# Quad 5 of a sigmoid attention: transposes by DMA in place of TensorE, an earlier load, and a counted order of matmuls

## The chip, the cores and the metric

The kernel runs on one core of a Trainium2 chip. The metric is the device time of one launch in microseconds. The times given for the kernel before are three runs: 369.92 us median, from 369.61 to 370.37. A profiled execution is a run of its own, with a record of every instruction; it took 369.69 us, of which 367.7 us lie between its first and last instruction (its span). Times inside a profile are counted from the start of the span.

## The reference

Two layers, one after the other. Inputs are q, k and v (8 batches, 12 heads, 448 positions, 64 wide), `w_in` (768 x 2048) and `w_out` (2048 x 768), all float32.

```python
scores = scale * np.matmul(q, k.transpose(0, 1, 3, 2)) - np.log(S)   # S = 448, scale = 1/8
attn = 1.0 / (1.0 + np.exp(-scores))
attn_out = np.matmul(attn, v)
x = attn_out.transpose(0, 2, 1, 3).reshape(B * S, H * D)             # 3584 x 768
h = x @ w_in
g = h * (1.0 / (1.0 + np.exp(-h)))
out = g @ w_out
```

The attention has no row sum, so every score goes through a sigmoid alone. Per batch that is a small attention (12 heads) and then two dense products over 448 rows.

## The kernel before, in words

Data is held in float16 on the chip, sums in float32 in PSUM.

**Quads, rounds and units.** Four heads of one batch are a quad; a batch has three (`NQ`), the kernel 24, numbered g = 0 to 23. Batch 0 is quads 0 to 2, batch 1 quads 3 to 5. A quad's scores are computed in seven rounds (`NCH`), each over 64 of its 448 key positions per head. A unit is one (quad, round) pair, numbered n = 7 g + round, so quad 5 has units 35 to 41. `scores` (L218) is one unit: four matmuls into a double PSUM bank and one sigmoid on ScalarE (L232). There are two such double banks. `values` (L240) is 28 matmuls for a quad over two single banks, and two scaled copies on VectorE (L267) into `xT`.

**Transposed q and k.** Scores need q and k with the head dimension on partitions (`kT`, `qT`). There are two ways in the code. `pe_transpose` (L188) multiplies by an identity on TensorE: 14 matmuls per tensor (L196) into two PSUM banks, and two casts on VectorE (L203). `dma_transpose` (L207) makes a row copy (`kr`, `qr`, L211) and lets SP issue a transposing DMA (L212). Quads 0 to 5 use the first, quads 6 to 23 the second.

**Loads.** POOL issues all loads of q, k, v, `w_in` and `w_out` in program order, with a cast from float32. At most eight are outstanding: each new one waits for the landing of the one eight before it. A tensor's buffer (three each for kf, qf, vf) must have been read before it is loaded again. `after_transpose(g)` (L633) and `after_values(g)` (L645) issue what follows a quad's transposes and values: after quad 1's transposes k and q of quad 4 and the first two quarters of `w_in`, after quad 2's k and q of quad 5, after quad 5's those of quad 8. A quarter of `w_in` is four transfers (L155) and 512 of its 2048 columns: h chunks 4 to 7 read the second quarter.

**h.** `h_unit` (L284) computes one chunk of 128 columns of h for a batch by six matmuls (L288) in a single bank. In batch 0 ScalarE then takes a sigmoid (L302) and VectorE multiplies (L303, this frees the bank); in batch 1 ScalarE takes one SiLU (L307). There are four single banks, which h, values and TensorE's transposes share. The bank that was released longest ago is taken.

**Order of the work.** The order on every engine is the order in which Python issues the calls. Units 0 to 23 follow a table (`behind`, L696). From unit 24 on (`NT_B + 3`) there are bursts of two units (L738), with the values of a finished quad behind them, and between bursts steps of h from the generator `first_h` (L551): all 16 chunks of batch 0, then of batch 1. How many steps follow a burst is set by a clock: `stretch(stream, 1600)` (L728) adds 1600 ns to what is due and takes steps, each 189 ns by the `yield 189` of `h_unit`, until they are used up. That makes 9, 8, 9, 8 and so on, 85 in all. Before that, four steps each of chunks 0 and 1 are done in the table. The values of quads 3, 4 and 5 come at burst 28, at burst 36 and behind the last burst. Quad 5's k is transposed behind burst 26, its q behind burst 30:

```python
    for n in range(NT_B + 3, 2 * NT_B, 2):
        burst(n)
        if n in (26, 30):
            transposes(5, "k" if n == 26 else "q")
        stretch(stream, 1600)
```

The rest of h for batches 0 and 1 follows without interruption, with sums of `w_in` and `w_out` pieces on VectorE between (L326, L477) and the row copies and DMA transposes of quads 6, 7 and 8. Then come the output products of batches 0 and 1 (`out_set`, L487) mixed with the attention of batches 2 and 3, and so on in pairs of batches.

Of the kernel before, what the change touches and what calls it, by code (L numbers as in the profile page):

```python
# [17 lines left out]
def kernel(  # L18
# [9 lines left out]
    nc = tc.nc  # L28
# [9 lines left out]
    NT_B = NQ * NCH  # L38
# [50 lines left out]
    def one_bank(name):  # L89
        if "any" in banks:  # L90
            ring.append(ring.pop(0))
            return banks["any"].tile([P, 512], F32, tag=f"any{ring[-1]}", name=name)
        taken["single"] += 1
        return banks["single"].tile([P, 512], F32, tag="single", name=name)
# [16 lines left out]
    def new_flat(name, g):  # L111
        flat[name, g] = p3.tile([P, 2, NCH, D], F16, tag=f"{name}f", name=f"{name}f")

    def rows_in(name, g):
        b, iq = divmod(g, NQ)
        return source[name][b, 4 * iq : 4 * iq + 4].rearrange(
            "(i h) (p c) d -> (h p) i (c d)", h=2, c=NCH
        )

    def load(names, g, c0=0, c1=NCH):  # L120
        for name in names:
            if (name, g) not in flat:
                new_flat(name, g)
            nc.gpsimd.dma_start(  # L124
                flat[name, g][:, :, c0:c1].rearrange("p i c d -> p i (c d)"),
                rows_in(name, g)[:, :, c0 * D : c1 * D],
            )
# [22 lines left out]
    def load_w_in(step):  # L150
        cols = slice(step * DFF // 4, (step + 1) * DFF // 4)
        rows = moe_w_in[:, cols].rearrange("(iq j h d) f -> h j d iq f", j=2, h=2, d=D)
        for half in range(2):
            for j in range(2):
                nc.gpsimd.dma_start(  # L155
                    w_in_sb[j * D : (j + 1) * D, half * NQ : (half + 1) * NQ, cols], rows[half, j]
                )
# [13 lines left out]
    def new_qkT(g):  # L171
        for name in ("k", "q"):
            qkT[name, g] = p3.tile([P, NCH, P], F16, tag=f"{name}T", name=f"{name}T")
# [14 lines left out]
    def pe_transpose(g, pieces=(("k", 0, 4), ("k", 4, NCH), ("q", 0, 4), ("q", 4, NCH))):  # L188
        if ("k", g) not in qkT:
            new_qkT(g)  # L190
        for name, c0, c1, *copy in pieces:
            dst = qkT[name, g].rearrange("p c t -> p (c t)")
            ptr = one_bank(f"ptr{name}")
            for c in range(c0, c1):
                for j in range(2):
                    nc.tensor.matmul(  # L196
                        ptr[j * D : (j + 1) * D, (c - c0) * P : (c - c0 + 1) * P],
                        flat[name, g][:, j, c, :],
                        ident,
                        start=True,  # L200
                        stop=True,
                    )
            (copy[0] if copy else nc.vector.tensor_copy)(  # L203
                dst[:, c0 * P : c1 * P], ptr[:, : (c1 - c0) * P]
            )

    def dma_transpose(g, name, copy):  # L207
        if ("k", g) not in qkT:
            new_qkT(g)
        rows = p2.tile([P, NCH, 2, D], F16, tag=f"{name}r", name=f"{name}r")  # L210
        copy(rows, flat[name, g].rearrange("p j c d -> p c j d"))  # L211
        nc.sync.dma_start_transpose(  # L212
            out=qkT[name, g], in_=rows.rearrange("p c j d -> p (c j d)")
        )
# [59 lines left out]
    def first_col(m):  # L274
        return P if m % 2 == 0 else 0

    def room_x():
        return p3.tile([P, NQ, S], F16, tag="tx", name="tx")
# [5 lines left out]
    def h_unit(b, fc):  # L284
        ph = one_bank("ph")
        for at, cc in enumerate(pairs):
            assert b in ready or at < 4
            nc.tensor.matmul(  # L288
                ph[:, :S],
                w_in_sb[:, cc, fc * P : (fc + 1) * P],  # L290
                xT[b][:, cc, :],
                start=(at == 0),
                stop=(at == NCC - 1),
            )
            if at < NCC - 1:
                yield 189
        if fc == NFC - 1:
            h_done.add(b)
        to = gTr[:, fc, first_col(0) + b * S : first_col(0) + (b + 1) * S]
        if b == 0:  # L300
            tsig = room_x()[:, 0]
            nc.scalar.activation(tsig, ph[:, :S], AF.Sigmoid, bias=0.0, scale=ISX)  # L302
            nc.vector.scalar_tensor_tensor(  # L303
                out=to, in0=ph[:, :S], scalar=ISX, in1=tsig, op0=ALU.mult, op1=ALU.mult
            )
        else:
            nc.scalar.activation(to, ph[:, :S], AF.Silu, bias=0.0, scale=ISX)  # L307
        yield 189
# [236 lines left out]

    by_h1 = {3: 6, 6: 7, 9: 8}
    early = [h_unit(0, fc) for fc in range(2)]
    sums = w_sums()
    in_sums = w_in_sums()

    def first_h():  # L551
        for b in range(2):
            for fc in range(NFC):
                yield from early[fc] if b == 0 and fc < 2 else h_unit(b, fc)
                if b == 0 and fc >= 10 or b == 1 and fc < 6:
                    next(in_sums)
                if b == 0:
                    continue
                if fc >= 2:
                    next(sums)  # L560
                if fc in by_h1:
                    for name in ("k", "q"):
                        dma_transpose(by_h1[fc], name, nc.vector.tensor_copy)
                    if by_h1[fc] == 8:

                        nc.gpsimd.tensor_copy(gate, qkT["q", 8][:1, 0, :1])
                        for to in (9, 10, 11):
                            load("kq", to)

    def sets(m):  # L570
        for g in range(0, NCH - 1, 2):
            step = out_set(
                block(m, g), row_blocks(m, g), block(m, g + 1), row_blocks(m, g + 1)
            )
            for i, ns in enumerate(step):
                if m == 0 and g == 0 and i in (10, 14):
                    next(sums)
                if m == 0 and g == 0 and i in (20, 28, 36, 44):
                    next(in_sums)
                yield ns  # L580
        if m % 2 == 1:
            g = NCH - 1
            yield from out_set(
                kept, row_blocks(m - 1, g), block(m, g), row_blocks(m, g), m == B // 2 - 1
            )
# [47 lines left out]
    def after_transpose(g):  # L633
        if g == 0:
            load("kq", 3)
        elif g == 1:
            load("kq", 4)
            load_w_in(0)
            load_w_in(1)
        elif g == 2:  # L640
            load("kq", 5)
        elif g == 5:
            load("kq", 8)

# [20 lines left out]
    def values_if_any():  # L665
        if waiting:
            g = waiting.pop(0)
            values(g)
            after_values(g)
            return True  # L670
        return False
# [6 lines left out]
    def rest_of_first_k():  # L678
        pe_transpose(0, (("k", FIRST, 4), ("k", 4, NCH)))
        after_transpose(0)  # L680

    def transposes(g, name):
        pe_transpose(g, ((name, 0, 4), (name, 4, NCH)))
        if name == "q":
            after_transpose(g)
# [37 lines left out]
        for do, *what in behind.get(n, ()):  # L723
            do(*what)

    done = due = 0.0

    def stretch(stream, ns, spent=0):  # L728
        nonlocal done, due
        due += ns  # L730
        done += spent
        while done < due:
            step_ns = next(stream, None)
            if step_ns is None:
                return
            done += step_ns

    def burst(n, size=2):  # L738

        new = units[n : n + size]  # L740
        for u in new:
            scores(*u)
        with_values = values_if_any()
        for g, ch in new:
            if ch == NCH - 1:
                waiting.append(g)
                if 9 <= g + 3 < NQB:
                    later.extend(((g + 3, "k"), (g + 3, "q")))
        return with_values

    stream = first_h()
    stretch(stream, 1600)
    for n in range(NT_B + 3, 2 * NT_B, 2):
        burst(n)
        if n in (26, 30):
            transposes(5, "k" if n == 26 else "q")
        stretch(stream, 1600)
    values_if_any()
    for _ in stream:
        pass  # L760
# [4 lines left out]
    for m in range(B // 2 - 1):  # L765
        banks_for_attention(3)
        nc.scalar.activation(warm, bias_s, AF.Sigmoid)
        stream = sets(m)
# [8 lines left out]
        left, n = 0.0, 2 * NT_B * (m + 1)  # L777
        for size in sizes * (2 * NQ):
# [3 lines left out]
            count = max(1, round(left / DENSE))  # L782
# [58 lines left out]
```

## Time and profile before

| | us |
|---|---|
| median of 3 runs | 369.92 |
| profiled execution | 369.69 |
| its span | 367.7 |
| 0 to 27.3: start, units 0 to 23 | 27.3, TensorE busy 24.3 |
| 27.3 to 56.6: bursts 24 to 40, values 3 to 5, h between | 29.3, TensorE busy 28.5, ScalarE 25.2 |
| 56.6 to 75.6: rest of h of batches 0 and 1 | 19.0, TensorE busy 18.9, VectorE 16.0 |
| 75.6 to 367.7: output products, attention and h of batches 2 to 7 | 292.1 |

The page names the engines PE (TensorE), DVE (VectorE), ACT (ScalarE), POOL and SP. A timeline row gives start, length, engine, line, instruction, what it writes and reads, and in brackets the idle time ahead of it with what ended that. A row of a view by windows gives the stretch, then each engine's busy time with the number of instructions, the granted clock of TensorE, the mean busy share of the 16 DMA engines (packets overlap, so that full engines show more than 1), and GB/s. A tile view gives the length of a DMA's issue and the time from the start of the issue to its landing.

### The profile page before, as it was taken

How to read it: one execution, taken by the hardware profiler on the slowest of the kernel's cores; microseconds unless marked ns; L12 is line 12 of the kernel's file. 1: busy time of each engine (PE TensorE's matmuls, PEld its weight loads, DVE VectorE, ACT ScalarE, POOL GpSimd, SP SyncE). 2: the span in 40 equal slices, each digit the busy share in tenths (PEclk: the TensorE clock that was granted, in tenths of full speed). 3: DMA queues.
4: the chain of work that ended last, by engine and by line, in shares of the span. 5: the costliest groups of instructions: out<-in, count | busy, mean ns of one | idle time of the engine just before them, and what ended most of it. 6: DMA issues, size and time to landing. Idle time of an engine off the chain costs nothing. (4 is left out here: it accounts for less than half of the span.)

```text
span 367.7 us, 7596 instructions
## 1 busy us (share of the span) xinstructions
PE 359.5 (98%) x3009; PEld 183.2 (50%) x3009; DVE 251.9 (68%) x458; ACT 249.9 (68%) x339; POOL 77.8 (21%) x116
## 2 busy tenths in 40 slices
PE   7999999999999999999999999999999999999995
PEld 2554445545544555544444545554455545555553
DVE  2565569867657587867665758795756667797763
ACT  5998885479998755687777846679998856640000
POOL 8566521040060172000051047000100000000000
PEclk9999999999999999999999999999999999999999
DMA  8999999989969499007589369912863020003333
GB/s 142 200 202 202 204 204 203 187 116 141 164 100 227 110 128 180 2 0 166 92 165 206 61 128 144 128 15 51 153 111 86 21 69 0 3 0 86 87 86 86
DMA packets 65698, 42.78 MB, mean 116 GB/s; under 512 B 36096, under 2 KB 62208, under 8 KB 65664
## 3 DMA queue, kind: packets, MB, share of 16 engines
q0 software_dynamic: 27072, 22.58, 42.3%
q1 hardware_dynamic: 38240, 19.44, 26.8%
q8 instruction: 23, 0.38, 0.4%
q10 hardware_dynamic: 352, 0.30, 0.2%
q14 instruction: 11, 0.09, 0.1%
HBM read 45.61 MB, written 11.01 MB: 154 GB/s over the span
## 5 line engine op out<-in xcount | busy, mean ns | idle before, releaser
L232 ACT ACTIVATE attnT<-psc,bias_s 128x896 f16<-128x896 f32 x168 | 158.1, 1009 | 21.9 <-PE psc L225 21.6
L504 PEld LDWEIGHTS <-S 128*128 128x128 f16 x448 | 41.3, 98 | 36.5 <-issue 8.1
L225 PE MATMUL psc<-qT,kT 64*64 64x448 f16 x672 | 51.1, 362 | 1.5 <-ACT qT L186 0.6
L267 DVE TENSOR_SCALAR xT<-pav 128x448 f16<-128x448 f32 x48 | 27.7, 620 | 33.2 <-PE pav L256 33.2
L124 POOL DMA_DIRECT2D vf<-in_v_dram x24 | 17.2, 717 | 135.0 <-PE pav L256 120.9
L504 PEld LDWEIGHTS <-gTr 128*128 128x128 f16 x336 | 31.3, 98 | 26.6 <-issue 7.7
L504 PE MATMUL po<-T,S 128*128 128x384 f16 x224 | 42.0, 327 | 0.2 <-DVE S L515 0.2
L504 PE MATMUL po<-w_out_sb,gTr 128*128 128x384 f16 x224 | 41.6, 327 | 0.0
L378 PEld LDWEIGHTS <-w_in_sb 128*128 128x128 f16 x288 | 27.7, 98 | 26.9 <-issue 1.7
L504 PE MATMUL po<-w_out_sb,S 128*128 128x384 f16 x224 | 40.8, 326 | 0.0
L256 PE MATMUL pav<-attnT,vf 64*64 64x448 f16 x672 | 38.9, 350 | 0.5 <-DVE gTr L303 0.4
L288 PE MATMUL ph<-xT,w_in_sb 128*128 128x448 f16 x192 | 38.7, 353 | 0.1
L378 PE MATMUL pa<-xT,w_in_sb 128*128 128x448 f16 x144 | 33.2, 353 | 0.0
L225 PEld LDWEIGHTS <-kT 64*64 64x64 f16 x672 | 17.8, 104 | 28.8 <-issue 22.3
L378 PEld LDWEIGHTS <-SI 128*128 128x128 f16 x216 | 21.1, 98 | 20.0 <-issue 0.5
L256 PEld LDWEIGHTS <-vf 64*64 64x64 f16 x672 | 21.0, 106 | 14.0 <-issue 4.7
L288 PEld LDWEIGHTS <-w_in_sb 128*128 128x128 f16 x192 | 17.8, 98 | 19.1 <-issue 3.7
L394 ACT ACTIVATE part<-pa 128x448 f32<-128x448 f32 x24 | 13.1, 544 | 19.9 <-PE pa L378 19.0
L504 PE MATMUL po<-T,gTr 128*128 128x384 f16 x112 | 22.1, 327 | 0.0
L372 ACT ACTIVATE gTr<-pc 128x448 f16<-128x448 f32 x24 | 13.1, 544 | 12.9 <-DVE pc L388 12.5
L388 DVE TENSOR_TENSOR part<-pb,part 128x448 f32<-128x448 f32 x24 | 14.9, 621 | 8.3 <-ACT part L394 5.0
L186 ACT ACTIVATE m<-po 128x384 f32<-128x384 f32 x1 | 0.5, 491 | 27.7 <-PE po L504 27.7
(75 smaller groups left out, 467.7 us busy)
## 6 DMA issues: line engine op xcount, KB each, us to landing
out_dram<-osb SPq DMA_DIRECT2D x54, 192.0 KB, 3.0
vf<-in_v_dram POOLq DMA_DIRECT2D x24, 224.0 KB, 7.0
kf<-in_k_dram POOLq DMA_DIRECT2D x23, 224.0 KB, 7.7
qf<-in_q_dram POOLq DMA_DIRECT2D x23, 224.0 KB, 7.9
w_in_sb<-in_moe_w_in_dram POOLq DMA_DIRECT2D x16, 192.0 KB, 8.2
w_out_sb<-in_moe_w_out_dram POOLq DMA_DIRECT2D x4, 768.0 KB, 14.9
kT<-kr SPq DMA_TRANSPOSE x18, 4.1
qT<-qr SPq DMA_TRANSPOSE x18, 4.8
```

Source lines behind the costliest of these rows:

```text
L124: nc.gpsimd.dma_start(flat[name, g][:, :, c0:c1].rearrange("p i c d -> p i (c d)"), rows_in(name, g)[:, :, c0 * D : c1 * D],)
L186: nc.scalar.activation(o, i, AF.Copy)
L225: nc.tensor.matmul(psc[own, j, :S], qkT["k", g][rows, ch, own], qkT["q", g][rows, :, own], start=True, stop=True,)
L232: nc.scalar.activation(attnT[g, ch], psc[:, :, :S], AF.Sigmoid, bias=bias_s, scale=QKSCALE)
L256: nc.tensor.matmul(pav[half][j * D : (j + 1) * D, :S], flat["v", g][own, j, ch, :], at[own, j, :], start=(ch == 0), stop=(ch == NCH - 1),)
L267: nc.vector.tensor_scalar_mul(xT[b][:, half * NQ + iq, :], pav[half][:, :S], SX)
L288: nc.tensor.matmul(ph[:, :S], w_in_sb[:, cc, fc * P : (fc + 1) * P], xT[b][:, cc, :], start=(at == 0), stop=(at == NCC - 1),)
L372: nc.scalar.activation(gTr[:, r * NG + i, col + c * S : col + (c + 1) * S], h, AF.Silu, bias=0.0, scale=ISX)
L378: nc.tensor.matmul(to, w[:, n, i * P : (i + 1) * P], x[:, n], start=(start and n == 0), skip_group_check=not start, stop=(n == NQ - 1),)
L388: nc.vector.tensor_add(o, po, x)
L394: nc.scalar.activation(got[i, 1], bank[i, "a"], AF.Copy)
L504: nc.tensor.matmul(po[:, :NO2], a[:, fc, :], w[:, fc, :], start=(fc == 0), stop=(fc == NHC - 1))
```

## The change

Three edits, all in batch 1.

- The two loads of quad 5 (k and q) are issued by POOL ahead of the second quarter of `w_in`, which moves from `after_transpose(1)` to `after_transpose(2)`.
- Quad 5's transposes leave TensorE. Behind burst 24 k's row copy comes after the first step of h and q's after the fifth (`i in (0, count // 2)` with count 9), each followed by a transposing DMA. `after_transpose(5)`, which loads quad 8, follows that burst. On POOL this places quad 8's loads ahead of v of quad 6.
- The steps of h are counted: 8 ahead of burst 24, then 9, 12, 4, 9, 9, 12, 4, 8 and 9 behind the nine bursts, 84 in all. `stretch` and the 189 ns go.

```diff
@@ h_unit
-                yield 189
+                yield
@@ after_transpose
         elif g == 1:
             load("kq", 4)
             load_w_in(0)
-            load_w_in(1)
         elif g == 2:
             load("kq", 5)
+            load_w_in(1)
@@ the bursts of batch 1
-    done = due = 0.0
-
-    def stretch(stream, ns, spent=0):
...
     stream = first_h()
-    stretch(stream, 1600)
-    for n in range(NT_B + 3, 2 * NT_B, 2):
+    for _ in range(8):
+        next(stream)
+    for n, count in zip(range(NT_B + 3, 2 * NT_B, 2), (9, 12, 4, 9, 9, 12, 4, 8, 9)):
         burst(n)
-        if n in (26, 30):
-            transposes(5, "k" if n == 26 else "q")
-        stretch(stream, 1600)
+        for i in range(count):
+            next(stream)
+            if n == NT_B + 3 and i in (0, count // 2):
+                dma_transpose(5, "q" if i else "k", nc.vector.tensor_copy)
+        if n == NT_B + 3:
+            after_transpose(5)
     values_if_any()
```

The function that it now calls for quad 5:

```python
    def dma_transpose(g, name, copy):
        if ("k", g) not in qkT:
            new_qkT(g)
        rows = p2.tile([P, NCH, 2, D], F16, tag=f"{name}r", name=f"{name}r")
        copy(rows, flat[name, g].rearrange("p j c d -> p c j d"))
        nc.sync.dma_start_transpose(
            out=qkT[name, g], in_=rows.rearrange("p c j d -> p (c j d)")
        )
```

More of the change, by code (lines that the diff above doesn't have):

```diff
@@ L724 @@
             do(*what)
-    done = due = 0.0
-    def stretch(stream, ns, spent=0):
[L729 to L736, printed above, removed]
     def burst(n, size=2):
```

## The prediction

> **What bounds the kernel now.** I read the page first, then TensorE's timeline through batch 1, then ScalarE's and VectorE's timelines of the same stretch, then the tile views of single transfers. The page says who sets the time:
>
> ```profile
> PE 359.5 (98%) x3009; PEld 183.2 (50%) x3009; DVE 251.9 (68%) x458; ACT 249.9 (68%) x339; POOL 77.8 (21%) x116
> ...
> PE 48%; DVE 0%; issue 0%
> ```
>
> TensorE is busy for 359.5 of 367.7 us, and the chain of waits runs on it. A microsecond gained or lost on TensorE in batch 1 goes through to the end as long as the next stages wait for nothing new. Cut into stages, the stretch that changes (27.3 to 56.6 us) holds most of TensorE's idle time outside the two ends:
>
> ```profile
> core 0: us, PE busy (x) PEld busy (x) DVE busy (x) ACT busy (x) POOL busy (x), PEclk, DMA share, GB/s
> 27.30:56.60 29.30, 28.49 (x277) 13.22 (x273) 16.06 (x29) 25.19 (x35) 13.12 (x19) 1.00 1.28 203
> 56.60:75.60 19.00, 18.93 (x104) 9.72 (x101) 16.02 (x33) 9.99 (x17) 2.55 (x5) 1.00 1.09 175
> ```
>
> The clock is granted in full. ScalarE works 25.2 of 29.3 us, so it is nearly as full as TensorE, and the DMA engines move 203 GB/s without a pause. TensorE's timeline shows the steps (start, length, instruction, idle time before it):
>
> ```profile
> 27.32 2.74 PE L288 MATMUL ph<-xT,w_in_sb 128*128 128x448 f16 x13
> 29.99 0.57 PE L225 MATMUL psc<-qT,kT 64*64 64x448 f16 x8
> ...
> 32.75 0.41 PE L196 MATMUL ptrk<-ident,kf 128*64 128x128 f16 x8
> 33.53 0.36 PE L196 MATMUL ptrk<-ident,kf 128*64 128x128 f16 x6 [0.37 <-DVE gTr L303]
> ...
> 47.62 1.51 PE L256 MATMUL pav<-attnT,vf 64*64 64x448 f16 x26 [0.45 <-DVE gTr L303]
> ...
> 55.11 1.57 PE L256 MATMUL pav<-attnT,vf 64*64 64x448 f16 x28
> 56.61 19.12 PE L288 MATMUL ph<-xT,w_in_sb 128*128 128x448 f16 x99
> ```
>
> Both waits are for a PSUM bank that VectorE (L303) still reads. And the transfers that come closest to the new ones, three transposes from the tile views of single issues:
>
> ```profile
> L212 SPq DMA_TRANSPOSE kT<-kr x1: 1324/1324/1324, 62.8 to 62.8; - x1
> DMA to landing us min/median/max: 6.2/6.2/6.2
> ...
> L212 SPq DMA_TRANSPOSE qT<-qr x1: 2671/2671/2671, 134.2 to 134.2; - x1
> DMA to landing us min/median/max: 9.0/9.0/9.0
> ...
> L212 SPq DMA_TRANSPOSE qT<-qr x1: 2989/2989/2989, 223.3 to 223.3; - x1
> DMA to landing us min/median/max: 12.7/12.7/12.7
> ```
>
> A transpose on an idle DMA takes 3.0 us; beside loads 6 to 13.
>
> **Removed from TensorE.** Quad 5's 28 transpose matmuls go. The block of 14 at 39.58 ends with the next h at 40.09: 0.51 us. Two blocks: 1.02 us. With them go the 0.37 us wait inside the first, and on VectorE four casts (two pairs of 1.15 us) for two row copies of 0.61 us each, the length of kr and qr at 62.04. VectorE has idle time here (16.1 of 29.3 us busy), so that swap is free.
>
> **The new order of h.** A step of h costs 0.202 us (9 in 1.81), a burst of two score units 0.50 (0.40 ahead of values), values 1.43; on ScalarE two sigmoids of scores take 1.80 and one of h 0.43. I walked the new order from 27.32 with these, holding each matmul for its bank and each sigmoid for ScalarE's order. The same walk over the old order puts the bursts within 0.16 us of the trace and the end of h at 75.47 (trace: 75.57). In the new order the bursts begin at 29.75, 32.06, 34.98 (values at 35.85 after 0.37 of wait), 38.09, 40.41, 42.72, 45.80 (values at 46.44, 0.13 of wait), 48.67 and 50.79. The last values are reached at 53.11, but their second bank is that of h chunk 13, whose sigmoid now stands behind the scores of the last burst: L303 frees it at 54.35, 1.24 us of wait. So the old waits (0.58 in the walk for the 0.37 above, 0.74 for the 0.45, 0.32 for the xT of values 5 at 57.95) are 1.64 us, the new ones 1.90 with 0.16 at unit 35: the count order moves waits more than it removes them. Sum: -1.02 - 1.64 + 1.90 = -0.76 by the terms, -0.79 by the ends of the two walks (75.47 to 74.68, rounding of the steps between). One h step more is left behind the last values (100 for 99); it is in the walk. Ends for the waits: none of the new ones comes (-1.02 - 1.26 = -2.3; 1.26 is what the old trace really has: 0.37, 0.45, 0.22 at 57.95 and 0.22 by which the bursts at 32.11 and 44.02 are stretched to 0.71 and 0.65), or they come a third larger (-0.2).
>
> **The transfers.** kr is behind two L303 on VectorE and starts at 30.5; its transpose leaves SP 0.1 us after the copy, as at 62.75: 31.2. qr starts at 33.1 behind chunk 2's L303, its transpose leaves at 33.8. SP has nothing else until 62.75. Scores of quad 5 want both in the second half of the burst at 42.72, at 42.97. So qT may take 9.2 us and kT 11.7. The nearest rows by stage are 6.2 and 5.5 (62.75, 64.17: five loads outstanding, at 203 GB/s); with loads that go on being issued, 7.1 to 9.0 (five of the six transposes from 129 to 140 us) and 7.1 to 12.7 (five of six from 218 to 230); the first of each six met no load and took 3.0 and 2.9. I take 9 for both, the upper end of the rows in which k and q come in pairs beside one to four loads: qT lands at 42.8, just hidden, at no cost. If that cover is gone, each microsecond over 9.2 stops TensorE for one. Ends: 0 and 12.7 - 9.2 = 3.5 us.
>
> Whether a transpose stands behind the loads issued before it or shares the engines with them decides this. The rows look like standing behind: kT at 62.75 lands at 68.9, when the last of the loads then outstanding has landed at 68.0. Sharing gives the same there, because no load followed. The q transpose of 130.7 tells more: one load was outstanding, which landed at 135.4, and it still took 7.7 us beside a load issued after it, so it shared. I take sharing; standing behind, qT would follow v 4 and the first w_out load (issued at 34.02, landed at 44.95) and the sum would be -0.8 + (44.95 - 42.97) = +1.2 or more, which is a case of the first rival below. [...]
>
> **Loads moved.** On POOL quad 5's two loads pass four of w_in's: they leave at about 18.2 and 19.1 (their buffers are free when quad 2's transposes end at 18.1 and 18.9) and not at 21.8 and 23.1, so they land near 26, well ahead of 30.5. w_in's second quarter lands two slots later, at 30.6 where it was 28.7 (the slots of old kf and qf: 29.5 and 30.6); h needs its first half at 31.9 and the second at 32.1 or later. Cost 0, and 1.3 us of cover. Quad 8's loads pass v 6, which is wanted after 78 us: 0. The two transposes move 448 KB on engines that are full. At 195 GB/s, the mix of loads and transposes at 144 to 145.5, this pushes every later load back by 2.3 us; at the 139 GB/s of 221 to 226 by 4. The tightest are v 5 (49.9, wanted at 54.35), the last w_out (57.7, wanted by VectorE's sums at 59.8) and the row copies behind transposes 6 (VectorE waited 1.05 us for these at 69.03 already). VectorE then has 3.25 us of idle time before 77.08. At 2.3 us all of it is covered; at 4 about 0.7 is lost. I take 0, and 0.7 for the upper end.
>
> **Sum.** -0.8 + 0 + 0 = -0.8 on the profiled run's own 369.69 us (span 367.7 and 2.0 around it). That run is 0.23 below the median of the three, 369.92. I forecast 369.1 against that median.
>
> **Rivals.** *The transpose of q is late (slower).* Place: the ldweights of L225 at unit 35. Price: what qT takes beyond 9.2 us, and it decides from 10.0. For it: the 9.7 to 12.7 of 221 to 230, and that here the stream of loads never pauses. Against: 6.2 and 5.5 at the same 203 GB/s. At 12.7: -0.8 + 3.5 = +2.7, 372.6. *A wait takes the gain (no change).* Bank waits a third larger, or VectorE late by the loads pushed back: -0.8 + 0.7, 369.8. For it: ScalarE at 25.2 of 29.3 us, nine sigmoid pairs that cannot start earlier; against: the walk met the old bursts. *The waits dissolve.* If bank releases come earlier than I walked, 1.1 more is gained: 368.0. Against: the last one follows from ScalarE's order alone.
>
> [...]
>
> **How the numbers follow.** Hidden 0.50, late 0.25, no change 0.15, dissolved 0.10. Under 0.2% (0.74 us) a measurement of this kernel can hardly tell a change. The hidden case, with 368.4 to 369.7 as its own range, is beyond that bound by a little and in 6 of 10; with the dissolved case: faster 0.42. The rest of hidden, most of no change and short delays: same 0.30. Late, with small shares of others: slower 0.28. The range leaves out the far halves of the outer cases: 367.8 to 372.0.
>
> **What would show it.** Right: no idle before L225 at unit 35 near 43 us, kT and qT of quad 5 landing in 9 us, last values at about 54.4 after a wait for L303, first po of the next stage near 74.8. Wrong: L225 waiting for DMA qT, or VectorE's S sums after 76 with TensorE waiting for them.

## The result and the profile after

The changed kernel takes 374.55 us (median of 4 runs, 374.18 to 375.37) against 370.02 us for the kernel before (4 runs). The ratio is 1.0126, with an interval from 1.0114 to 1.0138: slower by 4.5 us, where 0.8 us less was forecast, and outside the range given (up to 372.0). The profiled execution is the longest of the four, 375.37 us with a span of 373.3; for before the span was 367.7.

The page of the changed kernel: engine, busy time, share and instructions, and one line from its groups of instructions.

```profile
PE 360.7 (97%) x2981; PEld 182.8 (49%) x2981; DVE 250.7 (67%) x456; ACT 249.9 (67%) x339; POOL 77.5 (21%) x116
...
L225 PE MATMUL psc<-qT,kT 64*64 64x448 f16 x672 | 51.5, 365 | 4.9 <-DMA qT<-qr 3.2
```

TensorE has 28 matmuls fewer and is busy for 1.2 us *more*, and scores waited 3.2 us for a DMA into qT. TensorE's timeline of the changed stretch (start, length, instruction, idle time before it and its end):

```profile
27.34 2.55 PE L288 MATMUL ph<-xT,w_in_sb 128*128 128x448 f16 x12
29.82 0.57 PE L225 MATMUL psc<-qT,kT 64*64 64x448 f16 x8
...
36.03 1.51 PE L256 MATMUL pav<-attnT,vf 64*64 64x448 f16 x26 [0.26 <-DVE gTr L303]
...
42.96 0.38 PE L225 MATMUL psc<-qT,kT 64*64 64x448 f16 x4
46.53 0.59 PE L225 MATMUL psc<-qT,kT 64*64 64x448 f16 x4 [3.18 <-DMA qT<-qr]
47.05 4.66 PE L288 MATMUL ph<-xT,w_in_sb 128*128 128x448 f16 x12
51.64 0.90 PE L225 MATMUL psc<-qT,kT 64*64 64x448 f16 x8
...
60.38 1.51 PE L256 MATMUL pav<-attnT,vf 64*64 64x448 f16 x26 [0.82 <-DVE gTr L303]
61.82 19.09 PE L288 MATMUL ph<-xT,w_in_sb 128*128 128x448 f16 x100
80.75 2.44 PE L504 MATMUL po<-w_out_sb,gTr 128*128 128x384 f16 x14
```

Up to 42.96 the bursts stand within 0.3 us of the forecast (42.72). Then unit 35 stops for 3.18 us, and the twelve steps of h behind it take 4.66 us. The same twelve take 2.44 us at full clock. The view by windows says why (stretch, busy time and instructions of each engine, granted clock, DMA share, GB/s):

```profile
43.40:45.50 2.10, 0.00 (x0) 0.00 (x0) 0.62 (x1) 1.28 (x2) 0.24 (x1) 1.00 1.28 191
45.50:52.30 6.80, 5.77 (x24) 2.17 (x28) 1.71 (x3) 2.00 (x4) 0.72 (x1) 0.50 1.31 203
52.30:56.00 3.70, 3.70 (x49) 1.60 (x42) 2.09 (x4) 3.33 (x4) 1.43 (x2) 0.99 1.32 205
```

TensorE stopped at 43.34. Some 2.2 us later the granted clock fell to half, and it stayed there until 52.3, for 6.8 us, most of them after the work had resumed. The tile views of the two transposes (issue length and start, then time from issue to landing):

```profile
L212 SPq DMA_TRANSPOSE kT<-kr x1: 1326/1326/1326, 31.2 to 31.2; - x1
DMA to landing us min/median/max: 10.6/10.6/10.6
...
L212 SPq DMA_TRANSPOSE qT<-qr x1: 3102/3102/3102, 33.9 to 33.9; - x1
  PE psc L225: 3.2, 1
DMA to landing us min/median/max: 12.5/12.5/12.5
```

Both left SP when forecast, and both landed late: qT at 46.39.

The difference of the two profiled spans is 5.6 us. The first output product starts at 80.75 where it was 75.57 (+5.18), and what follows takes 0.4 us longer (292.5 for 292.1). Of the 5.18, the pause is 3.18. The half clock after it is 2.76: h from 47.05 to 51.64 takes 4.59 us for 2.38, the scores around it 0.52 for 0.31 and 0.74 for 0.40. The rest, 5.18 - 3.18 - 2.76, is -0.76, close to the -0.8 that was forecast for everything else.

### The profile page after: what moved, and what is told of

It reads as the page before. It is cut to its first block, busy times and chain, and to the rows that moved or that the text cites. A ratio compares the mean times of both kernels' runs of the same rounds, so it can differ in the third digit from the quotient of the medians.

```text
span 373.3 us, 7543 instructions
## 1 busy us (share of the span) xinstructions
PE 360.7 (97%) x2981; PEld 182.8 (49%) x2981; DVE 250.7 (67%) x456; ACT 249.9 (67%) x339; POOL 77.5 (21%) x116
## 5 line engine op out<-in xcount | busy, mean ns | idle before, releaser
L288 PE MATMUL ph<-xT,w_in_sb 128*128 128x448 f16 x192 | 40.7, 367 | 0.0
L372 ACT ACTIVATE gTr<-pc 128x448 f16<-128x448 f32 x24 | 13.1, 544 | 12.9 <-DVE pc L388 12.5
L303 DVE SCALAR_TENSOR_TENSOR gTr<-ph,tx 128x448 f16<-128x448 f32 x16 | 9.7, 621 | 16.1 <-ACT tx L302 16.1
```

The costliest lines, as they stand in the source:

```text
L288: nc.tensor.matmul(ph[:, :S], w_in_sb[:, cc, fc * P : (fc + 1) * P], xT[b][:, cc, :], start=(at == 0), stop=(at == NCC - 1),)
L303: nc.vector.scalar_tensor_tensor(out=to, in0=ph[:, :S], scalar=ISX, in1=tsig, op0=ALU.mult, op1=ALU.mult)
L372: nc.scalar.activation(gTr[:, r * NG + i, col + c * S : col + (c + 1) * S], h, AF.Silu, bias=0.0, scale=ISX)
```

## Experiments

All kernels below compute the whole reference; two add matmuls of a dummy tile whose result nobody reads. Each is measured beside the kernel before on the same chip (370.07 to 370.15 us, 15 to 25 runs). Diffs are against the changed kernel unless the text says otherwise.

### Is the clock a cost of its own?

`keep_busy(15)` puts 15 dummy matmuls on TensorE at the place of the wait. They shorten nothing; they only keep it from standing still.

```diff
+            if u == (5, 0):
+                keep_busy(15)
```

> The changed kernel with 15 dummy matmuls of 128x512 (0.21 us each) on TensorE between units 34 and 35, where it waits for q's transpose: the wait is filled with work, nothing is made earlier. Theory A: q still lands at about 46.4, unit 35 starts there, but the clock stays at 1.00 and the 12 steps of h behind it take 2.4 us and not 4.7: 2.3 us less than the changed kernel in its profiled run, 372.0 to 372.6 for the time. Rival C (the slow steps of h have another cause, such as the DMA traffic or the row copies): the steps stay at 0.37 us each and the time at 374.5.

Measured: 373.18 us (373.13 to 373.92, 4 runs), ratio 1.0090 [1.0075, 1.0105]. TensorE's timeline of this kernel:

```profile
43.70 3.41 PE L183 MATMUL pw<-dummy 128*128 128x512 f16 x15
...
47.36 2.44 PE L288 MATMUL ph<-xT,w_in_sb 128*128 128x448 f16 x12
```

qT landed as late as before (46.55), the twelve steps take 2.44 us again, and from the first h step of the stretch to the first output product it is 50.74 us (27.77 to 78.51) for 53.41. That is 2.67 us for the clock in the profiled runs. The medians differ by 1.4 only, less than expected; the profiled run of the changed kernel had the lowest clock of its four (a mean of 0.991, the others 0.993 and 0.994), so an ordinary run loses less. An estimate from these means: 6.8 us at half clock lower the mean of a 373 us run by 0.009, half as long by 0.0046, so the other three runs fit a fall half as long, which costs up to 1.7 us. Work that does nothing made the kernel faster: the clock is a cost of its own, of 1.4 to 2.7 us.

With half as many dummies the pause should become short enough to keep the clock:

```diff
+            if u == (5, 0):
+                keep_busy(7)
```

> The changed kernel with 7 dummy matmuls (1.5 us) ahead of unit 35 in place of 15: the same landing of q, the pause shortened from 3.2 to about 1.7 us. In the changed kernel's trace the clock fell 2.2 us after TensorE stopped. Theory A: 1.7 us are too short, the clock stays at 1.00 and the time is that of the run with 15, 372.5 to 373.5. If any idle time here drops the clock: 374 or more.

Measured: two runs, 372.92 and 375.65 us, the slower one profiled. In that one qT took 13.2 us and landed at 47.66, so the pause was still 2.26 us. TensorE's timeline, and the windows of the same run:

```profile
47.80 0.38 PE L225 MATMUL psc<-qT,kT 64*64 64x448 f16 x4 [2.26 <-DMA qT<-qr]
48.11 4.13 PE L288 MATMUL ph<-xT,w_in_sb 128*128 128x448 f16 x12
```

```profile
45.50:48.30 2.80, 0.54 (x6) 0.26 (x6) 0.00 (x0) 0.07 (x1) 0.00 (x0) 1.00 1.31 197
48.30:51.80 3.50, 3.50 (x11) 1.43 (x10) 1.10 (x2) 1.91 (x3) 0.71 (x1) 0.51 1.32 207
51.80:56.00 4.20, 4.20 (x55) 1.78 (x53) 2.51 (x6) 3.04 (x4) 1.43 (x2) 1.00 1.30 201
```

The clock fell here too, half a microsecond *after* TensorE had gone back to work, and for 3.4 us instead of 6.8. The other run kept a mean clock of 1.0 and was 2.7 us faster. How long it paused is not on record, so the two runs do not settle how long a pause must be to cost clock, and neither forecast is confirmed.

### Do the counts or the moved loads cost anything?

The counted order and the moved loads are kept; quad 5's transposes go back to TensorE behind bursts 26 and 30.

```diff
         burst(n)
+        if n in (26, 30):
+            transposes(5, "k" if n == 26 else "q")
-            if n == NT_B + 3 and i in (0, count // 2):
-                dma_transpose(5, "q" if i else "k", nc.vector.tensor_copy)
-        if n == NT_B + 3:
-            after_transpose(5)
```

> The counted order of h and the moved loads alone: quad 5 is transposed on TensorE behind bursts 26 and 30 as before. Theory A: the walk ends h at 75.43 against 75.47 for the order before, so no change: 369.6 to 370.4. Rival B: this order or these loads are what costs, 372 or more.

Measured: 370.17 us (369.49 to 370.57, 10 runs), ratio 1.0000 [0.9991, 1.0010], as expected. From the first h step to the first output product it takes 48.39 us, 48.25 before. These two parts together cost and bring nothing. This kernel also puts quad 8's loads back behind burst 30, but in the changed kernel these left at 52.93 and 53.84 us, behind the pause, so they cannot have caused it. The whole loss belongs to the DMA transposes.

The next kernel asks whether the waits for banks, which the prediction counted, are really worth what it gave for them. It is the kernel before (loads, and transposes on TensorE, as there) with counted steps, chosen so that no values wait for a bank. The diff is against the kernel before:

```diff
-    stretch(stream, 1600)
-    for n in range(NT_B + 3, 2 * NT_B, 2):
+    for _ in range(8):
+        next(stream)
+    for n, count in zip(range(NT_B + 3, 2 * NT_B, 2), (12, 6, 2, 8, 12, 9, 1, 9, 6)):
...
-        stretch(stream, 1600)
+        for _ in range(count):
+            next(stream)
```

> The kernel before, with TensorE's transposes and its own load order, and another counted order of h, found with the walk so that no bank and no sigmoid is waited for: 8, then 12, 6, 2, 8, 12, 9, 1, 9 and 6 (73 steps in place of 85, the rest behind the last values). Theory A (what TensorE waits for in this stretch are banks behind ScalarE's order, and the walk has them right): no wait over 0.1 us, h ends 1.8 us earlier than before (73.64 against 75.47); time 368.2 to 368.8, unless VectorE's sums then end too late. Rival F (ScalarE bounds the stretch, an order of steps gives nothing): 369.5 to 370.5.

Measured: 368.79 us (368.47 to 369.17, 5 runs), ratio 0.9968 [0.9956, 0.9981]: at the upper edge of what was expected, and faster than both kernels. TensorE's timeline:

```profile
51.29 1.52 PE L256 MATMUL pav<-attnT,vf 64*64 64x448 f16 x28
52.74 21.17 PE L288 MATMUL ph<-xT,w_in_sb 128*128 128x448 f16 x111
74.55 2.44 PE L504 MATMUL po<-w_out_sb,gTr 128*128 128x384 f16 x14 [0.63 <-ACT gTr L307]
```

No bank wait is left before values. A new wait of 0.63 us for the last SiLU gives a part back: h now ends so early that ScalarE is last.

### Do the loads make the transposes late?

If the transposes share the DMA engines with loads, they land earlier when fewer loads are outstanding. Here POOL holds back v of quad 5, `w_out` and the loads of quads 6 to 8 until qT has landed (`gate` is a small copy on POOL that reads qT):

```diff
         elif g == 5:
-            load("kq", 8)
+            nc.gpsimd.tensor_copy(gate, qkT["q", 5][:1, 0, :1])
+            load("v", 5)
+            load_w_out(0, 0)
+            load_w_out(0, 1)
+            load_w_out(1, 0)
+            load_w_out(1, 1)
+            for to in (6, 7, 8):
+                load("kq", to)
@@ after_values
             load("v", 4)
-            load_w_out(0, 0)
-            load_w_out(0, 1)
         elif g == 2:
-            load("v", 5)
-            load_w_out(1, 0)
-            load_w_out(1, 1)
-            load("kq", 6)
-            load("kq", 7)
+            pass
```

> The changed kernel with POOL's loads held back: w_out, v 5 and the loads of quads 6 to 8 are issued only after quad 5's q transpose has landed (a one-element copy on POOL reads qT). Nothing else moves; the transposes leave SP at 31.2 and 33.9 as in the changed kernel. Theory A (the transposes share the DMA engines with the stream of loads at 40 to 47 KB per us): the last load ahead of the gate (v 4) lands near 42.6, about 334 of the 448 KB of transposes are through by then, the rest goes at the 220 KB per us of an idle DMA: q lands at 43.2 to 43.8 and not 46.4, TensorE pauses under 0.6 us, the clock stays at 1.00. Time 369.3 to 370.8, as the held loads come later to VectorE's sums. Rival E (two transposes in a row are slow by themselves, or their issue on SP is): q lands at 46 or later, the pause and the slow steps stay, 374 or more.

Measured: 377.85 us (376.21 to 379.12, 4 runs), ratio 1.0198 [1.0175, 1.0220]. qT takes 10.0 us and lands at 44.02 instead of 46.39. TensorE's timeline:

```profile
44.16 0.38 PE L225 MATMUL psc<-qT,kT 64*64 64x448 f16 x4 [0.64 <-DMA qT<-qr]
44.47 2.44 PE L288 MATMUL ph<-xT,w_in_sb 128*128 128x448 f16 x12
...
75.62 2.44 PE L504 MATMUL po<-w_out_sb,gTr 128*128 128x384 f16 x14
79.76 0.57 PE L225 MATMUL psc<-qT,kT 64*64 64x448 f16 x8 [1.70 <-DMA qT<-qr]
```

The landing and the short pause came nearly as the theory has it (43.8 and 0.6 at most were expected), the clock stays full here, and the h phase is back at 75.62. kT took longer than in the changed kernel (11.9 us for 10.65), but the pair is through 12.6 us after k's issue, for 15.2. From 41 to 43 us, when the loads ran out, the transposes moved 85 GB/s, for 46 in the changed kernel from 40 to 44. The time did not come as expected, because the held loads are now late themselves: the last `w_out` landed at 67.26 (57.7 before), quad 6's scores wait 1.70 us for their q at 79.76, and the output products 4.2 us for VectorE's sums, once more with a lower clock (mean 0.991). What follows the h phase takes 301.7 us for 292.1. Part of this is the hold and not the sharing: from 38 to 48 us the engines moved 105 GB/s, for 204 before. But what the loads lose here is missing 30 us later.

The changed kernel's own DMA queues show how the engines are shared (queue, packets, MB, share of 16 engines' time; q0 carries the loads, q1 the transposes), from 37 to 44 us:

```profile
q0 software_dynamic: 1242, 1.03, 90.8%
q1 hardware_dynamic: 1245, 0.31, 34.0%
```

The two queues got nearly the same number of packets, 1242 and 1245. A load's packet is some 830 bytes here and a transpose's some 250, so the transposes got less than a quarter of the bytes. And they began late: k's transpose left at 31.23, and no packet of a transpose ran before 35.1. From 35.1 to 46.1 all 1856 of them ran, with 2000 of the loads.

### One tensor instead of two

k by DMA as in the change, q back on TensorE behind burst 30:

```diff
+        if n == 30:
+            transposes(5, "q")
-            if n == NT_B + 3 and i in (0, count // 2):
-                dma_transpose(5, "q" if i else "k", nc.vector.tensor_copy)
+            if n == NT_B + 3 and i == 0:
+                dma_transpose(5, "k", nc.vector.tensor_copy)
```

> The changed kernel with k of quad 5 transposed by DMA, q on TensorE behind burst 30. Theory A: with one transpose in flight k lands by 42 us at the latest (41.9 in the changed kernel), ahead of unit 35 at 43.5; no pause; the walk ends h at 74.91 against 75.47 before: 369.3 to 369.7. Rival D (a transpose beside this stream of loads is late by itself, one or two): k lands past 43.5 and TensorE pauses, 371 or more.

Measured: 370.17 us (369.53 to 370.43, 10 runs), ratio 1.0002 [0.9993, 1.0012]. kT took 10.1 us and landed at 41.77, no pause, no lower clock. The half microsecond of gain that was expected is missing. In the profile the stretch from the first h step to the output products is 48.01 us for 48.39 with both on TensorE, but it began at 27.80; that start lies anywhere from 26.92 to 27.92 in these kernels, so one profile cannot say more.

k earlier, behind unit 21, q on TensorE behind burst 24, with counts that leave no bank wait:

```diff
-        21: ((begin, 0, 4),),
+        21: ((begin, 0, 4), (dma_transpose, 5, "k", nc.vector.tensor_copy)),
...
-    for n, count in zip(range(NT_B + 3, 2 * NT_B, 2), (9, 12, 4, 9, 9, 12, 4, 8, 9)):
+    for n, count in zip(range(NT_B + 3, 2 * NT_B, 2), (9, 9, 2, 9, 10, 9, 2, 10, 4)):
         burst(n)
-        for i in range(count):
-            next(stream)
-            if n == NT_B + 3 and i in (0, count // 2):
-                dma_transpose(5, "q" if i else "k", nc.vector.tensor_copy)
         if n == NT_B + 3:
-            after_transpose(5)
+            transposes(5, "q")
+        for _ in range(count):
+            next(stream)
```

> k of quad 5 by DMA with its row copy behind unit 21, q on TensorE behind burst 24, loads moved as in the changed kernel, and a counted order without waits in the walk: 8, then 9, 9, 2, 9, 10, 9, 2, 10 and 4. Theory A: k leaves at 26.3 and lands by 37.7, unit 35 comes at 42.3, no pause; the walk ends h at 73.12, 2.3 us earlier than before. Of that a part is lost to VectorE's sums, for which the loads come about 1 us later: 367.7 to 368.8. Rival: the loads pushed back by the transpose take all of what the order gains over the run with TensorE's transposes: 368.8 or more.

Measured: 369.11 us (368.69 to 369.66, 11 runs), ratio 0.9976 [0.9968, 0.9985]. The rival held. TensorE's timeline shows the load that the transpose pushed back, v of quad 5, landed at 52.17 (49.6 where no transpose runs):

```profile
52.21 1.52 PE L256 MATMUL pav<-attnT,vf 64*64 64x448 f16 x28 [1.07 <-DMA vf<-in_v_dram]
```

Half the transposes are off TensorE, and the kernel is no faster than the one with new counts alone.

### Both tensors, but earlier

If lateness is the fault, an earlier start should mend it. First both 5 us earlier, k behind unit 21, q behind the values of quad 2:

```diff
-        21: ((begin, 0, 4),),
-        22: ((rounds, 2, 7),),
+        21: ((begin, 0, 4), (dma_transpose, 5, "k", nc.vector.tensor_copy)),
+        22: ((rounds, 2, 7), (dma_transpose, 5, "q", nc.vector.tensor_copy)),
```

> The changed kernel, but quad 5's two row copies come earlier on VectorE: k's behind unit 21, q's behind the values of quad 2, so that their transposes leave SP at about 26.7 and 29.0 us (31.2 and 33.9 in the changed kernel). Theory A (the q transpose lands late because two transposes in a row share full DMA engines with the loads, TensorE pauses at unit 35, and the pause halves its clock): k and q need 15.2 us from k's issue to q's landing, as in the changed kernel, so q lands at 41.9, ahead of the 43.2 at which unit 35 wants it; no pause, clock 1.00 throughout, h of batches 0 and 1 ends near 74.7 and the time is 0.5 to 0.8 below before: 369.2 to 369.5. Rival B (the counted order of h or the moved loads cost the time, or transposes beside loads slow TensorE anyway): still 372 or more.

Measured: 370.75 us (370.14 to 372.09, 10 runs), ratio 1.0024 [1.0012, 1.0036]: between the two forecasts. The profiled run is the fastest of the ten. q left 5.0 us earlier and landed only 3.0 us earlier, at 43.35, for it took 14.5 us. TensorE's timeline and the windows:

```profile
43.49 0.38 PE L225 MATMUL psc<-qT,kT 64*64 64x448 f16 x4 [0.22 <-DMA qT<-qr]
43.81 2.44 PE L288 MATMUL ph<-xT,w_in_sb 128*128 128x448 f16 x12
```

```profile
31.50:32.50 1.00, 1.00 (x12) 0.35 (x10) 0.00 (x0) 1.00 (x3) 0.18 (x1) 1.00 1.13 37
31.75:32.25 0.50, 0.50 (x7) 0.18 (x8) 0.00 (x0) 0.50 (x2) 0.00 (x0) 1.00 0.09 10
32.50:33.50 1.00, 1.00 (x9) 0.51 (x6) 0.88 (x2) 1.00 (x3) 0.00 (x0) 1.00 1.22 196
```

For one microsecond from 31.5 on the DMA engines moved 37 GB/s, with eight loads and two transposes outstanding. The busy share of 1.13 comes from the first quarter of it; in the middle, from 31.75 to 32.25, the share is 0.09, so hardly any packet was under way at all.

Then k behind unit 21 and q behind the first step of h after burst 24, to keep the two apart:

```diff
+        21: ((begin, 0, 4), (dma_transpose, 5, "k", nc.vector.tensor_copy)),
...
-            if n == NT_B + 3 and i in (0, count // 2):
-                dma_transpose(5, "q" if i else "k", nc.vector.tensor_copy)
+            if n == NT_B + 3 and i == 0:
+                dma_transpose(5, "q", nc.vector.tensor_copy)
```

> As the changed kernel, but k's row copy stands behind unit 21 (its transpose leaves at about 26.3 us, as in the run with both tensors early) and q's behind the first step of h after burst 24 (about 31.2). The two transposes are then 5 us apart and not 2.6. Theory (each transposed tensor takes 10 to 11.5 us beside the loads when the other does not overlap most of it; only lateness and the clock cost the changed kernel its time): k lands near 37.6, q at 41.5 to 42.7, just ahead of the 42.97 at which unit 35 asks for it; no pause, clock full, h ends 74.7 to 75.1, and the time is 369.2 to 369.8 (ratio 0.998 to 0.9995). Rival A (the loads that are pushed back take all that TensorE saves): no pause either, h ends as early, but the rest takes 292.9 us or more after it instead of 292.1, and the time is 370.0 or more. Rival B (a standstill of the DMA engines of about 1 us, as in the run with both tensors early, is part of running two transposes beside the loads): q lands at 43.5 or later, TensorE waits 0.5 to 1.5 us, 370.0 to 371.5.

Measured: 370.96 us (370.21 to 373.64, 10 runs), ratio 1.0028 [1.0011, 1.0045]. k landed at 37.71; q took 11.9 us, to 43.48, just as unit 35 wanted it. The standstill was there again (29 GB/s from 32.25 to 33.0). The profiled run, 371.75 us, is on the slow side of the ten. Rival A held: 294.1 us after the h phase instead of 292.1, with waits for VectorE's sums (0.3 us in two places) and for an output buffer that VectorE empties (1.1 us at 85.7). Of rival B the standstill and the late landing came (43.48, for 42.7 at most in the theory), but not its pause of 0.5 to 1.5 us: h began later in this run (27.77 for 27.34), so unit 35's burst did too, and it took 0.82 us for 0.57.

Last, the same with counts that avoid the bank waits, and v of quad 5 loaded ahead of the second `w_out` load (the diff is against the kernel just shown):

```diff
             load("v", 4)
             load_w_out(0, 0)
-            load_w_out(0, 1)
         elif g == 2:
             load("v", 5)
+            load_w_out(0, 1)
             load_w_out(1, 0)
...
-    for n, count in zip(range(NT_B + 3, 2 * NT_B, 2), (9, 12, 4, 9, 9, 12, 4, 8, 9)):
+    for n, count in zip(range(NT_B + 3, 2 * NT_B, 2), (9, 10, 2, 9, 10, 9, 2, 11, 2)):
```

> The same two places for the transposes, with the steps of h behind the bursts counted 9, 10, 2, 9, 10, 9, 2, 11, 2 (72 with the first 8), so that no values wait for a bank, and the load of v of quad 5 ahead of the second w_out load instead of behind it, so that pushed loads cannot hold up the last values. Unit 35 asks for q at about 42.9 to 43.1. Theory: no bank wait and no wait for v; h ends 73.4 to 74.0; the last w_out lands near 61, which costs 0.3 to 0.9 us after the h phase; 367.9 to 368.7, as fast as or a little faster than the kernel with new counts alone (368.8). Rival (transposes pushing the loads back cost as much as the 1.0 us of TensorE work that they take away): 368.8 to 369.6.

Measured: 370.86 us (369.79 to 373.59, 12 runs), ratio 1.0026 [1.0009, 1.0044]. Worse than either forecast. The profiled run, 369.94 us, is the second fastest of the twelve, so it shows less than the median's loss. TensorE's timeline:

```profile
43.27 0.38 PE L225 MATMUL psc<-qT,kT 64*64 64x448 f16 x4 [1.17 <-DMA qT<-qr]
...
74.41 2.44 PE L504 MATMUL po<-w_out_sb,gTr 128*128 128x384 f16 x14
...
78.53 1.31 PE L504 MATMUL po<-T,S 128*128 128x384 f16 x7 [0.75 <-DVE S L515]
```

qT took 12.1 us from 31.0 and is 1.17 us late, and the last `w_out`, 3.1 us later than before, holds up the sums for 0.75. h ends 1.2 us earlier than before, and the rest is 1.3 us longer (293.5). The two slowest of the twelve runs, 372.9 and 373.6, have a mean clock of 0.995 where the others have 0.997 to 1.0. They probably lost the clock for a while; these runs were not profiled, so it is not shown.

## Why the prediction was wrong

**Removed from TensorE: right, as far as shown.** 28 matmuls went. The kernel with the transposes put back takes 48.39 us from the first h step to the output products, the changed kernel 53.41 - 3.18 - 2.76 = 47.47 without pause and clock: 0.9 us less, for 1.02 forecast.

**The new order of h: right.** The bursts met the walk within 0.25 us as far as 42.96. The two bank waits it named are there, 0.26 us for 0.37 and 0.82 us for 1.24. They are shorter than walked, but so are the old ones: TensorE idles for 1.09 us of the stretch besides the pause, where it idled for 0.88 before, and the walk had 1.90 for 1.64. All that is neither pause nor clock comes to -0.76, against -0.8. The counted order alone is worth nothing (370.17 against 370.07), as the walk had it: it moves waits more than it removes them. The counts without bank waits gave 1.3 us, which the walk had not been asked for.

**The transfers: the step that failed.** It took 9 us for both transposes, "the upper end of the rows in which k and q come in pairs beside one to four loads". Measured were 10.65 and 12.52 us. The end it kept aside, 12.7 us and 3.5 us of pause, is what happened: 3.18 us. The choice of row was wrong by its own argument. The second six transposes that it named, 218 to 230, had one to four loads outstanding as well and took up to 12.7 us, so 9 was not the upper end of such rows; and the two rows that it read as free of loads had one outstanding for part of their 3 us. Here seven or eight loads are outstanding throughout (the prediction itself says that "the stream of loads never pauses"), and none of the rows that it leaned on has that.

It read correctly that the transposes share the engines with the loads, but left the sum at -0.8 and worked out no share. From 37 to 44 us of the changed kernel 1245 packets of the transposes ran beside 1242 of the loads, of some 250 bytes against 830: at 0.31 of 1.35 MB and 192 GB/s the transposes get 44 GB/s, at which the 0.46 MB of two tensors need 10.4 us, and 3.9 us pass before their first packet. That is 14.3 us, measured were 15.2 from k's issue to q's landing; the 11.7 us between k's issue and unit 35 did not suffice. That it is sharing is shown by the packet counts, by holding the loads back (q's 12.5 became 10.0 us) and by the early pair, where loads issued behind q's transpose landed ahead of it (one issued at 31.06, at 42.00; q, issued at 28.84, at 43.35). "Standing behind" the earlier loads is out.

**The clock: missing.** The prediction wrote "each microsecond over 9.2 stops TensorE for one". In truth the pause of 3.18 us cost another 1.4 to 2.7, shown by filling it with dummy matmuls. The rival "the transpose of q is late" therefore had its place and its condition right and its price too low: it gave 372.6, and with the clock's 1.4 to 2.7 it would have been 374.0 to 375.3, where the runs are.

**Loads moved: right in place, low in size.** The two loads came in time and moving them costs nothing. The pushback was forecast at 2.3 us, 4 at worst (448 KB at the 139 GB/s named there are 3.3 us, not 4); the last `w_out` came 3.4 us later (61.08 for 57.66), and v of quad 5 the same (53.30 for 49.89). In the changed kernel this costs only 0.4 us because the pause had delayed all that wants them by 5. Where the pause is short, what follows the h phase is longer by 0.9 (both early), 1.3 (spread, new counts) and 1.9 us (spread), or the last values wait 1.07 us. So the prediction's zero was wrong as well: even nearly punctual transposes had their gain taken back in these kernels, in which the standstill described below is part of the delay.

What was not shown: why some 4 us pass before a transpose's first packet here; how much of the 11.9 to 14.5 us that q takes when it leaves earlier is the standstill of the DMA engines; and the pause in the runs that were not profiled.

## What to carry to other kernels

Moving work from a full engine to the DMA did not pay here, where the DMA engines were full: 0.46 MB more on engines that moved 203 GB/s in this stretch of the kernel before, at a busy share of 1.28, came back as late transfers, late loads and a lower clock, and no variant with a DMA transpose was faster than the kernel with other step counts and everything else left alone (368.79 us; the nearest, 369.11, cannot be told from it). For a transfer's time beside others, take a row with as many transfers outstanding as there will be, or work out its share from the packets: here 1245 of the transposes, of some 250 bytes, ran beside 1242 of the loads, of some 830. And a forecast pause of TensorE is priced with the clock that may follow it, not by its length alone: in these profiles 2.26 and 3.18 us lost the clock, 1.70 us did not.

## What the runs showed that was not expected

**The clock falls and recovers in steps.** In the changed kernel it was half for 6.8 us (45.5 to 52.3), in the run with seven dummies for 3.4 us (48.35 to 51.77), one twice the other, and the fall came 2.2 us after TensorE stopped in one and 2.8 us after in the other, when it was already at work again. A pause of 2.26 us was enough. The 3.41 us ahead of each fall, a stretch about as long as the shorter of the two, in the changed kernel, the run with seven dummies and the one with held loads (there the fall was from 84.05 to 90.88, 6.8 us again):

```profile
42.12:45.53 3.41, 1.22 (x9) 0.40 (x7) 0.81 (x2) 2.56 (x4) 1.28 (x2) 1.00 1.28 192
44.94:48.35 3.41, 1.15 (x9) 0.39 (x8) 0.06 (x1) 0.43 (x2) 0.20 (x1) 1.00 1.30 196
80.64:84.05 3.41, 0.13 (x1) 0.00 (x0) 3.41 (x8) 1.46 (x2) 0.00 (x0) 1.00 0.83 154
```

TensorE was busy for 1.22, 1.15 and 0.13 us of them. With held loads it was busy for 1.71 us of the stretch before that (77.23 to 80.64, with the pause of 1.70 us), and the clock stayed full. Whether it is the busy time ahead that counts, and if so where between 1.22 and 1.71 us the limit lies, these traces do not show.

**The DMA engines stood nearly still for about a microsecond in five of the profiles.** In all four kernels with k's transpose behind unit 21 they moved some 10 to 75 GB/s, by quarters of a microsecond, for 0.75 to 1 us between 31.5 and 33.5, five to six microseconds after k's transpose left, with loads outstanding; one of the four has a single transpose, so it does not take two. In the run with seven dummies the same came at 42.0 (54 GB/s from there to 42.75). The changed kernel's profile has none there: from 27 to 47 us no half microsecond is below 182 GB/s. The cause is open.
